# Opening of a DiT block: single first loads, plus-one by a ones matmul, scaling from PSUM, another statistics order

## The chip, the cores and the metric

The kernel runs on one core of one Trainium2 chip. The metric is the device time of one execution in microseconds (us); lower is better. The profile's "span" runs from the first to the last instruction and is about 1.8 us shorter than the device time. The engines are called PE (TensorE matmul), PEld (its weight load), DVE (VectorE), ACT (ScalarE), POOL (GpSimd) and SP (SyncE, which here issues most of the loads).

Ratios in this document are the mean time of one kernel's fast runs over the mean time of the other's fast runs of the same rounds on the same chip, so they are not quite the ratio of the medians that are quoted beside them. The bracket after a ratio is its 95% interval.

## The reference, cut to what matters

```python
B, N, D = 2, 256, 1152
mod = (silu(c) @ w_mod).reshape(B, 6, 1, D)
shift_a, scale_a, gate_a, shift_m, scale_m, gate_m = [mod[:, i] for i in range(6)]
h = layernorm(x) * (1 + scale_a) + shift_a        # the opening: this line
qkv = (h @ wqkv)...                               # K first in this kernel
...                                               # attention, wo, second norm, MLP: untouched
```

All data are bf16. The 512 tokens are four tiles of 128: tiles 0 and 1 are batch 0, tiles 2 and 3 are batch 1. The 1152 features are nine chunks of 128.

## The kernel before

x is loaded by batch, each load 576 KB. The first group of attention-scale weights (two chunks) and then rows of the K weights follow on the same queue.

```python
for b in range(B):
    nc.sync.dma_start(x_sb[:, b * TPB:(b + 1) * TPB, :], x_v[:, b, :, :])
...
for g, (k0, k1) in enumerate(KGROUPS):            # (0,2) (2,4) (4,6) (6,9)
    load_scale_group(g, nc.sync)
    for k in range(k0, k1):
        nc.sync.dma_start(w_k[:, k, 0:KM1 * P], wqkv_v[:, k, D:D + KM1 * P])
```

DVE computes the statistics of tiles 0, 2 and 3 in three pieces each. ACT computes those of tile 1 by two passes over it (Identity, then Square). The normalised tile is transposed on PE into PSUM and scaled on its way out by 1 + scale; the result feeds the K matmuls. The scale itself comes from 18 small matmuls into a PSUM tile `pm`, and ACT adds the one:

```python
def scale_group(g):
    ...
    for j in range(k0, k1):
        for k in range(KD):
            nc.tensor.matmul(pm[:, j - k0, :], w_scale_a[...], sT[:, k, 0:B],
                             start=(k == 0), stop=(k == KD - 1))
    def add_one(eng):
        ...
        nc.scalar.activation(dst, pm[:], ACT.Identity, bias=one_t[:])
```

The instructions are written in the order in which each engine is to take them (`"a"` is ACT, `"d"` is DVE; `warm(n)` issues n matmuls on zeros, whose result nobody reads, so that PE is not idle):

```python
warm(12, pwarm)
act_stats(ACT.Identity, dsum)                     # ACT, tile 1
for j in range(NPD):
    stats_piece(0, j)                             # DVE, tile 0
sqrt1(0)                                          # ACT
act_stats(ACT.Square, dsq)                        # ACT, tile 1
stats_piece(2, 0)
recip1(0)
norm1(0, 0, CUT, "d")
stats_piece(2, 1)
pt_0 = transpose_x([0, 1], [0])
warm(4, pwarm)
act_stats_finish()
sqrt1(T_ACT)
stats_piece(2, 2, False)
recip1(1)
norm1(1, 0, CUT, "d")
stats_aggregate(2)
norm1(0, CUT, D, "d")
scale_group(0)("a")
for k in range(2):
    modulate(pt_0, k, k, 0, 0, P, "a")
warm(1, pwarm)
...                                               # transposes of tile 1 and of chunks 2, 3
k_step(0, 0, P)                                   # K matmuls on tile 0
k_step(1, 0, P)
stats_piece(3, 0)
recip1(2)
norm1(2, 0, CUT, "d")
k_step(0, P, N)                                   # K matmuls on tile 1
k_step(1, P, N)
...
for k in range(2):
    transpose_into(pt_1, 6 + k, k, 2)             # transposes of tile 2
```

## Time and profile before

| | before |
|---|---|
| device time, median (range, runs) | 244.01 us (243.85 to 244.24, 3) |
| span in the profile | 242.1 us |
| PE busy | 235.3 us, 97% of the span |
| first scale weights landed | 9.09 us |
| first K matmul | 10.49 us |
| first matmul of the full-width K panels (the "mark" below) | 26.26 us |

From the page of the kernel before: the busy time of each engine, the granted PE clock in 40 slices (9 is full speed), the shares of the chain that ended last, and the group of K matmuls of the opening (count, busy us, mean ns of one, idle before).

```profile
PE 235.3 (97%) x1698; PEld 142.7 (59%) x1698; DVE 93.4 (39%) x209; ACT 69.5 (29%) x138; POOL 32.0 (13%) x48
...
PEclk9999999999999999999999999999999999999999
...
PE 91%; DMA 3%; ACT 2%; DVE 2%; issue 0%; SPq 0%; DVEq 0%
...
L288 PE MATMUL pk<-big,w_k 128*128 128x128 bf16 (+2 forms) x102 | 13.3, 278 | 0.0
```

PE bounds the kernel. A change to the opening can therefore only slide everything behind it. How the opening hangs together is seen in the chain of waits of the kernel before, in order of time (start us, duration us, what).

```profile
1.66 7.42 DMA w_scale_a<-in_w_mod_dram
...
9.13 0.62 PE pm L248 x18
...
9.77 0.27 ACT scale_a L258
...
10.07 0.64 ACT big L275 x2
10.71 0.47 DVE big L273 x2
11.17 0.47 DVE stats L188
...
11.74 0.42 DVE xn L235
...
12.21 0.28 PE pt L358 x2
12.49 0.43 PE pm L248 x18
...
12.95 1.94 PE pk L288 x21
```

The weights' landing at 9.09 us comes first, then the scale matmuls, plus-one, scaling of chunks, a piece of DVE statistics, and from 12.21 us PE runs on. The timeline of the same kernel (start us, duration us, engine, line, operation, out<-in, count, and in brackets the idle time before it and what ended it) has the DVE side.

```profile
4.79 1.48 DVE L188 BATCH_NORM_STATS2 stats<-x_sb 128x6 f32<-128x384 bf16 x3 [3.64 <-DMA x_sb<-in_x_dram]
5.05 1.24 ACT L203 ACTIVATE xn<-x_sb 128x1152 bf16<-128x1152 bf16 x1
...
6.58 0.29 ACT L219 ACTIVATE rstd<-mv,eps_t 128x1 f32<-128x1 f32 x1 [0.19 <-DVE mv L193]
...
8.95 0.41 DVE L235 TENSOR_SCALAR xn<-x_sb,mv,rstd 128x512 bf16<-128x512 bf16 x1
...
9.13 0.60 PE L248 MATMUL pm<-sT,w_scale_a 128*128 128x2 bf16 x18 [0.41 <-DMA w_scale_a<-in_w_mod_dram]
...
10.09 0.49 PE L358 MATMUL pt<-ident,xn 128*128 128x128 bf16 x6
...
10.49 1.50 PE L288 MATMUL pk<-big,w_k 128*128 128x128 bf16 x24
...
12.21 0.28 PE L358 MATMUL pt<-ident,xn 128*128 128x128 bf16 x2 [0.22 <-DVE xn L235]
```

The first statistics wait for x at 4.79 us. Tile 1 is normalised at 8.95 us, before the weights land. Within the opening, the longest wait of PE after 10.5 us is the 0.22 us before tile 2's transposes.

### The profile page before, as it was taken

To read this page: it belongs to the slowest core of one execution; us is meant where nothing else is said; L and a number is where in the kernel's file an instruction comes from. 1 tells how busy PE (TensorE), PEld (TensorE's weight loads), DVE (VectorE), ACT (ScalarE), POOL (GpSimd) and SP (SyncE) were. 2 spreads that over 40 slices of the span, in tenths; PEclk is the share of its full clock that TensorE was granted. 3 is DMA by queue.
4 is the path that set the end of the run, shared out by engine and by line. 5 is a ranking of instruction groups with operands and counts; after the bars stand their busy time and mean duration, and the time that the engine had idled before them with its cause. 6 is when DMAs were issued, how large, how long until landed. Compare 5 with 4: busy or idle time off the path is not lost.

```text
span 242.1 us, 4031 instructions
## 1 busy us (share of the span) xinstructions
PE 235.3 (97%) x1698; PEld 142.7 (59%) x1698; DVE 93.4 (39%) x209; ACT 69.5 (29%) x138; POOL 32.0 (13%) x48
## 2 busy tenths in 40 slices
PE   8799999999999999999999999999999999999994
PEld 2486444466656666888844444444566656665573
DVE  2872550675694676720000019999002000000001
ACT  6532250543735174782222233322000000000000
POOL 1000400000310616300000000000314111111111
PEclk9999999999999999999999999999999999999999
DMA  6999999999999999799999999996891000000000
GB/s 223 324 330 360 379 344 247 326 372 284 254 322 361 380 255 208 208 219 327 327 328 249 191 274 328 327 326 188 245 286 39 19 16 16 20 20 27 19 19 16
DMA packets 76989, 54.48 MB, mean 225 GB/s; under 512 B 26011, under 2 KB 72491, under 8 KB 76971
## 3 DMA queue, kind: packets, MB, share of 16 engines
q1 hardware_dynamic: 76240, 53.02, 77.7%
q0 software_dynamic: 704, 1.20, 1.6%
q8 instruction: 13, 0.21, 0.4%
q14 instruction: 5, 0.04, 0.0%
q10 hardware_dynamic: 27, 0.00, 0.0%
HBM read 46.90 MB, written 1.19 MB: 199 GB/s over the span
## 4 chain that ended last, share of the span: by engine, by line
PE 91%; DMA 3%; ACT 2%; DVE 2%; issue 0%; SPq 0%; DVEq 0%
PE pacc L866 29%; PE pacc L802 29%; PE pacc L584 7%; PE pacc L705 6%; PE pacc L511 5%; PE pk L288 4%; DMA w_scale_a<-in_w_mod_dram 3%; PE pacc L519 2%; PE pk L318 2%; ACT hT L687 2%; PE pa L619 1%; PE ps_s L539 1%; PE pn L432 1%; PE pm L248 1%; PE pt L266 1%; PE pg L467 1%
## 5 line engine op out<-in xcount | busy, mean ns | idle before, releaser
L802 PE MATMUL pacc<-hT,w_f 128*128 128x256 bf16 (+1 forms) x432 | 70.5, 326 | 0.2 <-ACT hT L687 0.2
L866 PE MATMUL pacc<-w_f,gT 128*128 128x384 bf16 (+2 forms) x468 | 70.5, 314 | 0.0
L866 PEld LDWEIGHTS <-gT 128*128 128x128 bf16 x468 | 44.4, 98 | 26.2
L802 PEld LDWEIGHTS <-w_f 128*128 128x128 bf16 x432 | 42.2, 98 | 28.0 <-issue 0.4
L485 DVE SCALAR_TENSOR_TENSOR late<-w_gate_mT,late 128x1152 bf16<-128x1152 bf16 x18 | 24.4, 1358 | 36.8 <-DMA w_gate_mT<-in_w_mod_dram 36.2
L872 DVE TENSOR_TENSOR tmp<-pacc,gate 128x384 f32<-128x384 f32 (+2 forms) x13 | 6.8, 527 | 62.5 <-PE pacc L866 50.5
L840 ACT ACTIVATE gT<-pacc 128x512 bf16<-128x512 f32 x24 | 14.3, 597 | 32.3 <-PE pacc L802 32.3
L485 DVE SCALAR_TENSOR_TENSOR s_spill<-w_scale_m,s_b 128x1152 bf16<-128x1152 bf16 x12 | 16.3, 1357 | 8.5 <-DMA w_scale_m<-in_w_mod_dram 8.2
L705 PE MATMUL pacc<-w_o,big 128*128 128x384 bf16 (+2 forms) x117 | 17.9, 314 | 0.0
L874 POOL TENSOR_TENSOR o_sb<-tmp,x 128x384 bf16<-128x384 f32 (+1 forms) x12 | 11.7, 974 | 47.4 <-DVE tmp L872 47.4
L584 PE MATMUL pacc<-w_v,hT 128*128 128x384 bf16 x108 | 17.9, 326 | 0.0
L705 PEld LDWEIGHTS <-big 128*128 128x128 bf16 x117 | 11.0, 98 | 6.8 <-ACT big L627 0.2
L584 PEld LDWEIGHTS <-hT 128*128 128x128 bf16 x108 | 10.4, 98 | 7.0 <-issue 0.2
L288 PE MATMUL pk<-big,w_k 128*128 128x128 bf16 (+2 forms) x102 | 13.3, 278 | 0.0
L711 POOL TENSOR_TENSOR x<-tmp,x_sb 128x384 f32<-128x384 f32 (+1 forms) x11 | 9.8, 891 | 17.4 <-DVE tmp L710 9.5
L511 PE MATMUL pacc<-hT,w_q 128*128 128x512 bf16 x54 | 11.8, 379 | 0.1
L327 POOL DMA_DIRECT2D gates_dram<-grow x4 | 2.1, 521 | 70.8 <-DVE grow L826 70.8
L818 ACT ACTIVATE gT<-pacc 128x512 bf16<-128x512 f32 x12 | 6.9, 597 | 10.4 <-PE pacc L802 10.4
L288 PEld LDWEIGHTS <-w_k 128*128 128x128 bf16 x102 | 7.8, 98 | 3.0
L511 PEld LDWEIGHTS <-w_q 128*128 128x128 bf16 x54 | 5.3, 98 | 6.7 <-issue 0.4
L710 DVE TENSOR_TENSOR tmp<-pacc,gate 128x384 f32<-128x384 f32 (+2 forms) x13 | 6.7, 522 | 5.4 <-PE pacc L705 5.2
L523 ACT ACTIVATE big<-pacc 128x512 bf16<-128x512 f32 x9 | 4.8, 608 | 11.5 <-PE pacc L511 8.8
(101 smaller groups left out, 160.9 us busy)
## 6 DMA issues: line engine op xcount, KB each, us to landing
w_f<-in_w_fc_dram SPq DMA_DIRECT2D x14, 864.0 KB, 11.0
w_f<-in_w_fc_dram SPq DMA_DIRECT2D x2, 2592.0 KB, 10.7
w_f<-in_w_fc_dram SPq DMA_DIRECT2D x2, 1728.0 KB, 13.8
w_shift_a<-in_w_mod_dram SPq DMA_DIRECT2D x3, 864.0 KB, 10.5
w_v<-in_wqkv_dram SPq DMA_DIRECT2D x3, 864.0 KB, 6.0
w_gate_a<-in_w_mod_dram SPq DMA_DIRECT2D x3, 864.0 KB, 9.2
w_o<-in_wo_dram SPq DMA_DIRECT2D x3, 864.0 KB, 6.2
w_shift_m<-in_w_mod_dram SPq DMA_DIRECT2D x3, 864.0 KB, 13.0
```

What stands on the lines that cost most here:

```text
L288: nc.tensor.matmul(pk[m][:, c0:c1], w_k[:, k, m * P:(m + 1) * P], hT0[:, k, c0:c1], start=(k == 0 and c0 == 0), stop=(k == KD - 1), skip_g ...
L485: nc.vector.scalar_tensor_tensor(spill, wT[:, j, :], 1.0, s_b[b], op0=ALU.mult, op1=ALU.mult, accum_out=dst(j, b),)
L511: nc.tensor.matmul(pq[m][:], w_q[:, k, m * P:(m + 1) * P], hT[:, k, :], start=(k == 0), stop=(k == KD - 1),)
L584: nc.tensor.matmul(pacc[:], hT[:, k, t * P:(t + 1) * P], w_v[:, k, pnl * PW:(pnl + 1) * PW], start=(k == 0), stop=(k == KD - 1),)
L705: nc.tensor.matmul(pacc[:], aT[:, k, t * P:(t + 1) * P], w_o[:, k, c0:c1], start=(k == ks[0]), stop=(k == ks[-1]),)
L711: (nc.vector if (t, i) in ((1, 2), (3, 3)) else nc.gpsimd).tensor_tensor(x1[:, t, c0:c1], tmp[:], x_sb[:, t, c0:c1], op=ALU.add)
L802: nc.tensor.matmul(dst, w_f1[m // KD][:, k, ml * P:(ml + 1) * P], hT[:, k, c0:c1], start=(k == 0), stop=(k == KD - 1),)
L818: nc.scalar.activation(gT[:, ms[0]:ms[-1] + 1, b * N:(b + 1) * N], pacc[:], ACT.Gelu_apprx_tanh)
L840: nc.scalar.activation(gT[:, m, :], pacc[:], ACT.Gelu_apprx_tanh)
L866: nc.tensor.matmul(pacc[:], gT[:, kk, t * P:(t + 1) * P], w_f2[j][:, r, c0 - n * PW:c0 - n * PW + cw], start=(kk == 0), stop=(kk == KF - 1),)
L872: nc.vector.tensor_tensor(tmp[:], pacc[:], gate_m[:, b, c0:c0 + cw], op=ALU.mult)
L874: (nc.vector if last else nc.gpsimd).tensor_tensor(o_sb[:], tmp[:], x1[:, t, c0:c0 + cw], op=ALU.add)
```

## The change

The intent is to start the statistics of tile 0 earlier, because its half of the load lands first; to take ACT's plus-one out of the chain by seeding the PSUM tile with ones, so that the scale matmuls add onto them; and to let DVE scale the first chunks straight from that PSUM tile instead of waiting for ACT's copy. The order of statistics, transposes and K matmuls was rearranged with it.

```diff
@@ -81,8 +81,9 @@
     x_sb = act.tile([P, NT, D], BF16, name="x_sb", tag="x_in")
     c_sb = act.tile([B * KD, P], BF16, name="c_sb")
     nc.scalar.dma_start(c_sb[:], c_v)
-    for b in range(B):
-        nc.sync.dma_start(x_sb[:, b * TPB:(b + 1) * TPB, :], x_v[:, b, :, :])
+    for l in range(TPB):
+        nc.sync.dma_start(x_sb[:, l, :], x_v[:, 0, l, :])
+    nc.sync.dma_start(x_sb[:, TPB:NT, :], x_v[:, 1, :, :])
 
     zeros = const.tile([P, T], BF16, name="zeros")
     nc.vector.memset(zeros[:], 0.0)
@@ -90,8 +91,8 @@
     make_identity(nc, ident[:])
     eps_t = const.tile([P, 1], FP32, name="eps_t")
     nc.vector.memset(eps_t[:], LN_EPS)
-    one_t = const.tile([P, 1], FP32, name="one_t")
-    nc.vector.memset(one_t[:], 1.0)
+    ones_r = const.tile([1, P], BF16, name="ones_r")
+    nc.vector.memset(ones_r[:], 1.0)
     SW = 32
     sT = act.tile([P, KD, SW], BF16, name="sT")
     nc.gpsimd.memset(sT[:], 0.0)
@@ -240,24 +241,36 @@
 
     scale_a = act.tile([P, KD, B], FP32, name="scale_a")
 
-    def scale_group(g):
+    def scale_group_matmuls(g):
         k0, k1 = KGROUPS[g]
         pm = aux_tile([P, k1 - k0, B], "pm")
+        nc.tensor.matmul(
+            pm[:].rearrange("p j b -> p (j b)"), ones_r[:, 0:P], ones_r[:, 0:(k1 - k0) * B], start=True, stop=False,
+            skip_group_check=True,
+        )
         for j in range(k0, k1):
             for k in range(KD):
                 nc.tensor.matmul(
                     pm[:, j - k0, :], w_scale_a[:, k, j * P:(j + 1) * P], sT[:, k, 0:B],
-                    start=(k == 0), stop=(k == KD - 1),
+                    start=False, stop=(k == KD - 1), skip_group_check=True,
                 )
 
-        def add_one(eng):
+        return pm
+
+    def scale_group_copy(g, pm):
+        k0, k1 = KGROUPS[g]
+
+        def copy_out(eng):
             dst = scale_a[:, k0:k1, :]
             if eng == "d":
-                nc.vector.tensor_scalar_add(dst, pm[:], 1.0)
+                nc.vector.tensor_copy(dst, pm[:])
             else:
-                nc.scalar.activation(dst, pm[:], ACT.Identity, bias=one_t[:])
-
-        return add_one
+                nc.scalar.copy(dst, pm[:])
+
+        return copy_out
+
+    def scale_group(g):
+        return scale_group_copy(g, scale_group_matmuls(g))
 
     def transpose_x(ks, ts, pt=None, js=None):
         pt = aux_tile([P, len(ks), len(ts) * P], "pt", BF16) if pt is None else pt
@@ -330,28 +343,27 @@
 
     CUT = 4 * P
     warm(12, pwarm)
-    act_stats(ACT.Identity, dsum)
     for j in range(NPD):
         stats_piece(0, j)
+    act_stats(ACT.Identity, dsum)
     sqrt1(0)
     act_stats(ACT.Square, dsq)
-    stats_piece(2, 0)
     recip1(0)
     norm1(0, 0, CUT, "d")
-    stats_piece(2, 1)
+    for j in range(NPD):
+        stats_piece(2, j)
     pt_0 = transpose_x([0, 1], [0])
     warm(4, pwarm)
     act_stats_finish()
     sqrt1(T_ACT)
-    stats_piece(2, 2, False)
+    sqrt1(2)
+    stats_piece(3, 0)
     recip1(1)
     norm1(1, 0, CUT, "d")
-    stats_aggregate(2)
-    norm1(0, CUT, D, "d")
-    scale_group(0)("a")
+    pm_0 = scale_group_matmuls(0)
     for k in range(2):
-        modulate(pt_0, k, k, 0, 0, P, "a")
-    warm(1, pwarm)
+        nc.vector.tensor_scalar_mul(hT0[:, k, 0:P], pt_0[:, k, 0:P], pm_0[:, k, 0:1])
+    nc.scalar.copy(scale_a[:, 0:2, :], pm_0[:])
     pt_1 = aux_tile([P, 1, 8 * P], "pt", BF16)
 
     def transpose_into(pt, slot, k, t):
@@ -359,39 +371,41 @@
 
     for k in range(2):
         transpose_into(pt_1, k, k, 1)
-    for k in (2, 3):
-        for t in range(TPB):
-            transpose_into(pt_1, 2 * (k - 1) + t, k, t)
+    recip1(2)
+    norm1(2, 0, CUT, "d")
     for k in range(2):
-        modulate(pt_1, 0, k, 1, k * P, P, "d")
-    sqrt1(2)
+        modulate(pt_1, 0, k, 1, k * P, P, "a")
     k_step(0, 0, P)
     k_step(1, 0, P)
-    stats_piece(3, 0)
-    recip1(2)
-    norm1(2, 0, CUT, "d")
-    k_step(0, P, N)
-    k_step(1, P, N)
     stats_piece(3, 1)
     stats_piece(3, 2)
     for k in range(2):
         transpose_into(pt_1, 6 + k, k, 2)
+    k_step(0, P, N)
+    for k in (2, 3):
+        for t in range(TPB):
+            transpose_into(pt_1, 2 * (k - 1) + t, k, t)
+    k_step(1, P, N)
     for k in range(2):
         modulate(pt_1, 0, k, 2, (6 + k) * P, P, "a")
-    scale_group(1)("a")
     sqrt1(3)
-    for k in (2, 3):
-        modulate(pt_1, 0, k, 0, 2 * (k - 1) * P, N, "d")
     k_step(0, N, N + P)
-    k_step(1, N, N + P)
+    pm_1 = scale_group_matmuls(1)
     recip1(3)
     norm1(3, 0, CUT, "d")
+    for k in (2, 3):
+        nc.vector.tensor_scalar_mul(
+            hT0[:, k, 0:N], pt_1[:, 0, 2 * (k - 1) * P:2 * k * P], pm_1[:, k - 2, 0:1]
+        )
+    nc.scalar.copy(scale_a[:, 2:4, :], pm_1[:])
+    k_step(1, N, N + P)
     k_step(2, 0, N)
     k_step(3, 0, N, 0, 3)
     pt_4 = transpose_x([0, 1], [3])
     for k in range(2):
         modulate(pt_4, k, k, 3, 0, P, "d")
     k_step(3, 0, N, 3, KM1)
+    norm1(0, CUT, D, "d")
     norm1(1, CUT, D, "d")
     pt_5 = transpose_x([2, 3], [2, 3])
     for i, k in enumerate((2, 3)):
```

In words, for the order: DVE now does all of tile 2's statistics before those of tile 1 are finished; the two scalings of tile 0 go to DVE and those of tile 1 to ACT; and in PE's own queue the transposes of tile 2 move ahead of tile 1's K matmuls, and the four transposes of chunks 2 and 3 come between those K matmuls.

## The prediction

> **What bounds the kernel now.** TensorE. The page of before has PE busy 235.3 of 242.1 us, and 91% of the chain of waits is PE. The change touches only the opening. In the timeline PE does useful work without a gap from 12.2 us on, so every later stage simply slides with the opening. What can be won lies before that. In the chain the opening is: the first attention-scale weights land at 9.09 us (3.1% of the span); the scale matmuls run 9.13 to 9.73; ACT adds one (9.77 to 10.03) and scales two chunks (10.07 to 10.69); the first K matmuls start at 10.49; a DVE statistics, reciprocal and normalise piece holds PE idle 0.22 us until 12.21. The first matmul on chunk 2 comes at about 13.70 (12 K matmuls after 12.95). I compare that point, because the same PE work lies before it in both kernels.
>
> **What changes.**
> 1. x tile 0 lands alone. Half of a 576 KB load that landed at 4.75 us should land near 3.9. But the square root that tile 0 needs still stands on ACT behind the 1.24 us Identity pass over tile 1, which cannot start before 5.05 us (table load). So the root moves only from 6.58 to about 6.40: 0.18 us gained; DVE idles over a microsecond. The one more issue (0.41 us on SP) shifts the weights little: the DMA share is already near full there.
> 2. The plus-one goes to a ones matmul (tens of ns, ahead of the weights' landing for the first group; about 0.05 us each for later groups). The seeding is legal by the Trainium skill, "PSUM — Partial Sum Buffer", The four PSUM rules: matmuls without the first flag accumulate onto it. No run so far shows it.
> 3. DVE scales chunks 0 and 1 straight from PSUM. That takes ACT's 0.26 us out of the chain. But DVE now runs all three pieces of tile 2 (1.5 us) and their aggregate before tile 1's statistics. From root at 6.40: reciprocal 6.72, normalise 6.92, pieces 7.25 to 8.77, aggregate, three small operations 8.9 to 9.3, a tile 3 piece, reciprocal 9.8, normalise tile 1 9.97 to 10.38 (before: 8.95 to 9.36), the two scalings 10.30 to 10.78. So DVE, not the weights, ends the wait.
> 4. In the built program the tile 1 transposes, ahead of the K matmuls on PE, wait for those DVE scalings (buffer reuse); ACT's copy of the scale waits for DVE too, and tile 2's transposes wait for ACT's scalings of tile 1. I estimate first K matmul 10.95 (before 10.49), tile 2 transposes 11.8, scale group 1 at 13.4, chunk 2 at 14.1 to 14.4.
>
> **Sum.** +0.4 to +0.7 us at the comparison point, +0.1 for later ones matmuls, minus what my DVE chain overstates. The rest slides. I put it at +0.4 us: **244.4 us**, 8 in 10 between 243.7 and 244.9. Faster by over 2%: 1%; within 2%: 98%; slower by over 2%: 1%.
>
> **What would show it.** Timeline of after: first statistics near 3.9 instead of 4.79; DVE idle between tile 0's aggregate and its reciprocal near 6.7; normalise of tile 1 near 10.0; first K matmul later than 10.49; no ACT plus-one; PE continuous from about 13.4. All PE groups after 15 us unchanged in duration.
>
> **What would make it wrong.** Tile 0's square root getting in front of the Identity pass, which would pull the DVE chain forward by about a microsecond and give a gain of up to 0.5 us; x tile 1 landing after 5.05 us, or the scale weights after 10.3, which costs more; waits finer than I read them (tile 2's scalings released early), which brings the loss near zero.

## More of the kernel before

The mark is useful because all K work of the opening lies before it in both kernels and almost nothing after it changes.

The six transposes of tile 1 and of chunks 2 and 3 run at 10.09 us, ahead of the first K matmul, while PE waits for the scaled chunks.

## The result and the profile after

| | before | after |
|---|---|---|
| device time, median (range, runs) | 243.93 us (243.63 to 244.24, 4) | 246.79 us (246.53 to 246.98, 4) |
| span in the profile | 242.1 us | 245.2 us |
| first statistics | 4.79 us | 3.80 us |
| batch 1 of x landed | 6.22 us | 8.46 us |
| first scale matmul | 9.13 us | 10.49 us |
| first K matmul | 10.49 us | 12.12 us |
| the mark | 26.26 us | 29.60 us |

The ratio is 1.0116 [1.0099, 1.0134]. The loss is about 2.8 us where +0.4 us was predicted, and 246.79 us lies outside the predicted range. The mark moved by 3.34 us, and the first MLP matmul, far behind it, moved by 3.23 us (98.75 to 101.98 us): the loss is made in the opening, and the rest slides.

From the page of the kernel after: the engines, the granted clock and the group of K matmuls that answers to the one shown of before.

```profile
PE 237.5 (97%) x1701; PEld 144.5 (59%) x1701; DVE 93.8 (38%) x209; ACT 69.2 (28%) x138; POOL 31.9 (13%) x48
...
PEclk9979999999999999999999999999999999999999
...
L301 PE MATMUL pk<-big,w_k 128*128 128x128 bf16 (+2 forms) x102 | 14.7, 297 | 0.0
```

PE's busy time grew by 2.2 us with three more matmuls. Part of that is the same K matmuls taking longer (13.3 to 14.7 us), and the third slice of the clock shows a 7. The chain of waits of this execution reaches back only to 92.56 us, so the opening is read from the timeline of the kernel after.

```profile
3.80 1.48 DVE L189 BATCH_NORM_STATS2 stats<-x_sb 128x6 f32<-128x384 bf16 x3 [2.53 <-DMA x_sb<-in_x_dram]
...
4.98 1.24 ACT L204 ACTIVATE xn<-x_sb 128x1152 bf16<-128x1152 bf16 x1
...
6.53 0.16 DVE L223 RECIPROCAL rstd<-rstd 128x1 f32<-128x1 f32 x1 [0.98 <-ACT rstd L220]
...
8.48 1.48 DVE L189 BATCH_NORM_STATS2 stats<-x_sb 128x6 f32<-128x384 bf16 x3 [1.34 <-DMA x_sb<-in_x_dram]
...
10.49 0.60 PE L253 MATMUL pm<-sT,w_scale_a 128*128 128x2 bf16 x18 [1.90 <-DMA w_scale_a<-in_w_mod_dram]
...
11.15 0.41 DVE L236 TENSOR_SCALAR xn<-x_sb,mv,rstd 128x512 bf16<-128x512 bf16 x1
11.48 0.48 DVE L365 TENSOR_SCALAR big<-pt,pm 128x128 bf16<-128x128 bf16 x2
...
12.01 0.27 PE L370 MATMUL pt<-ident,xn 128*128 128x128 bf16 x2 [0.92 <-DVE big L365]
...
12.04 0.16 ACT L366 COPY scale_a<-pm 128x4 f32<-128x4 f32 x1 [1.02 <-DVE rstd L223]
...
12.12 0.83 PE L301 MATMUL pk<-big,w_k 128*128 128x128 bf16 x12
```

Three things are to be seen. The statistics of tile 0 do start earlier (3.80 us), and nothing comes of it: DVE waits 0.98 us for the root at 6.53 us, which stands on ACT behind the pass over tile 1. Then DVE waits 1.34 us for batch 1 of x, until 8.48 us, and PE waits 1.90 us for the scale weights, until 10.49 us: two landings that were predicted to stay where they were. And tile 1's normalisation (11.15 us) and the two DVE scalings stand between the scale matmuls and the first K matmul at 12.12 us. Of the two late landings it is batch 1's that counts in this execution: from 8.48 us until its scalings start at 11.48 us DVE goes from one instruction to the next with no wait over 0.1 us, and the scale matmuls had ended before that, at 11.09 us.

What the landing looked like, from the semaphore increments of the 16 DMA engines in the two traces (us, one number per increment; weights: first and last ones only):

```
before  batch 1 of x: 5.49 ... 5.91  6.08  6.22
before  scale weights: 7.57 ... 8.56  9.09
after   batch 1 of x: 5.39 5.44 5.49 5.50 5.52 5.53 5.54 5.56 5.80 5.84 5.89 6.04 6.09 7.42 8.29 8.46
after   scale weights: 7.37 ... 9.36  10.28  10.44
```

Thirteen of the 16 engines were done by 6.09 us; three came 1.3 to 2.4 us later, and the load counts as landed only with the last. The Trainium skill says so too, "DMA: Bandwidth & Descriptors", Why a DMA increments its semaphore by 16 and not by 1: only the full 16 means that all data landed; this trace agrees, DVE started at 8.48 us, 0.02 us after the sixteenth increment. While batch 1 was moving, two single 4608-byte packets took 1316 ns (started at 5.01 us) and 1519 ns (5.21 us), where the median is 178 ns. The trace does not name the engine of a packet, so that these two ran on late engines is not shown.

The granted clock is read in windows of 1 us. The columns are the window's start and end (us), its length, the busy share and count of PE, PEld, DVE, ACT and POOL, then the granted clock, the DMA share and GB/s. First the kernel before:

```profile
13.00:14.00 1.00, 1.00 (x15) 0.88 (x15) 0.97 (x5) 0.60 (x3) 0.00 (x0) 1.00 1.15 312
14.00:15.00 1.00, 1.00 (x13) 0.91 (x11) 0.44 (x2) 0.00 (x0) 0.00 (x0) 1.00 1.07 350
```

The windows of the kernel after:

```profile
9.00:10.00 1.00, 0.00 (x0) 0.00 (x0) 0.97 (x4) 0.00 (x0) 0.00 (x0) 1.00 1.13 339
...
11.00:12.00 1.00, 0.09 (x4) 0.10 (x1) 0.96 (x6) 0.03 (x1) 0.00 (x0) 1.00 1.01 293
...
13.00:14.00 1.00, 0.94 (x11) 0.94 (x11) 0.64 (x2) 0.00 (x1) 0.00 (x0) 0.62 1.17 316
14.00:15.00 1.00, 1.00 (x13) 1.00 (x10) 0.00 (x0) 0.61 (x3) 0.00 (x0) 0.50 1.01 313
15.00:16.00 1.00, 1.00 (x19) 0.79 (x18) 0.57 (x2) 0.20 (x2) 0.00 (x0) 0.50 1.00 310
16.00:17.00 1.00, 1.00 (x21) 0.97 (x19) 0.62 (x2) 0.00 (x0) 0.00 (x0) 0.67 1.03 320
```

PE is idle from 8.6 to 12.0 us but for the 0.60 us of scale matmuls, and from about 13.2 us it gets half its clock. If the clock is 1.00 or 0.50 and nothing between, the four shares make 0.76 + 1 + 1 + 0.66 = 3.42 us at half speed; one window laid over 13.24 to 16.66 us gives 0.50 for the whole of it. The Trainium skill, "TensorE: Matmul & The Clock Gate", Part 1: The HAM clock gate, describes this: a PE that was idle for a window of about 3.4 us gets 4 of 8 clock pulses until it has been busy for about 3.4 us, and the window runs freely, so that it varies between runs. The length and the factor agree with this trace. The condition does not quite: the longest waits of PE here are 1.90 and 0.92 us, and none is 3.4 us long.

### The profile page after: what moved, and what is told of

Read it like the earlier page. It is cut to its first block, busy times and chain, and to the rows that moved or that the text cites. A ratio compares the mean times of both kernels' runs of the same rounds, so it can differ in the third digit from the quotient of the medians.

```text
span 245.2 us, 4041 instructions
## 1 busy us (share of the span) xinstructions
PE 237.5 (97%) x1701; PEld 144.5 (59%) x1701; DVE 93.8 (38%) x209; ACT 69.2 (28%) x138; POOL 31.9 (13%) x48
## 4 chain that ended last, share of the span: by engine, by line
PE 57%; ACT 2%; DMA 1%; issue 0%; DVE 0%; ACTq 0%; DVEq 0%
PE pacc L880 29%; PE pacc L816 28%; ACT hT L701 2%; DMA hT<-xn 1%; ACT xn L680 0%; ACT rstd L671 0%; DVE tmp L886 0%; DVE o_sb L888 0%; ACTq L701 0%; DVEq L886 0%
## 5 line engine op out<-in xcount | busy, mean ns | idle before, releaser
L301 PE MATMUL pk<-big,w_k 128*128 128x128 bf16 (+2 forms) x102 | 14.7, 297 | 0.0
L301 PEld LDWEIGHTS <-w_k 128*128 128x128 bf16 x102 | 8.7, 107 | 2.8
L172 PE MATMUL pwarm<-zeros 128*128 128x512 bf16 x20 | 7.2, 524 | 1.2 <-DVE eps_t L93 1.2
## 6 DMA issues: line engine op xcount, KB each, us to landing
w_shift_a<-in_w_mod_dram SPq DMA_DIRECT2D x3, 864.0 KB, 11.1
```

The costliest lines, as they stand in the source:

```text
L172: nc.tensor.matmul(dst[:], zeros[:, 0:P], zeros[:], start=True, stop=True)
L301: nc.tensor.matmul(pk[m][:, c0:c1], w_k[:, k, m * P:(m + 1) * P], hT0[:, k, c0:c1], start=(k == 0 and c0 == 0), stop=(k == KD - 1), skip_g ...
```

## The experiments

Three theories stood against each other for the 2.8 us. *Loads*: the split first load makes batch 1 and the weights land late. *Order*: the rearranged instructions on DVE, ACT and PE are slower by themselves. *Clock*: the idle PE loses its clock. They are not exclusive, so the experiments were to size each. All kernels gave a correct result. Times are the median with range and number of fast runs; "at clock 1" means executions whose mean granted clock was 0.997 or more, and executions with the dip show 0.991 to 0.993. In each batch the kernel before was run on the same chip; its medians were 243.68, 243.79, 243.88, 243.82 and 243.63 us.

| experiment | what | median us (range, fast runs) | ratio [95%] |
|---|---|---|---|
| e1_split_only | before + split load | 245.41 (243.57 to 246.23, 6) | 1.0060 [1.0028, 1.0092] |
| e8_split_again | the same again, other chip | 244.99 (244.22 to 246.11, 4) | 1.0049 [1.0020, 1.0079] |
| e2_all_but_split | after with the loads of before | 245.65 (244.79 to 245.80, 6) | 1.0070 [1.0050, 1.0090] |
| e4_after_again | after, again | 246.41 (245.48 to 247.16, 4) | 1.0106 [1.0079, 1.0132] |
| e3_after_warm | after + warm matmuls | 245.45 (245.38 to 245.88, 5) | 1.0074 [1.0056, 1.0092] |
| e5_order_warm | e2 + warm matmuls | 245.08 (245.00 to 245.24, 6) | 1.0050 [1.0034, 1.0067] |
| e6_old_stats | e2, nearly old statistics order, warm | 245.27 (245.03 to 245.96, 6) | 1.0059 [1.0039, 1.0079] |
| e10_ones_only | before + ones matmul | 244.07 (243.87 to 244.40, 6) | 1.0008 [0.9990, 1.0026] |
| e11_stats_order_only | before + statistics order | 244.12 (243.76 to 244.23, 6) | 1.0007 [0.9990, 1.0023] |
| e9_psum_scale_old_order | before + ones + scaling from PSUM | 244.09 (243.82 to 244.90, 6) | 1.0015 [0.9995, 1.0034] |
| e13_pe_order_only | before + PE order | 244.75 (244.40 to 245.58, 6) | 1.0032 [1.0007, 1.0056] |
| e14_old_pe_order | e2 with the PE order of before | 244.97 (244.56 to 245.53, 5) | 1.0039 [1.0016, 1.0062] |
| e12_split_batch1 | before, batch 1 split | 244.00 (243.84 to 244.26, 4) | 1.0006 [0.9987, 1.0026] |
| e7_partition_halves | before, batch 0 in two halves of partitions | 245.06 (244.81 to 246.11, 4) | 1.0057 [1.0031, 1.0083] |
| e15_weights_first | before, weights ahead of batch 1 | 245.87 (244.32 to 246.67, 6) | 1.0072 [1.0039, 1.0104] |
| e16_split_weights_first | the same with batch 0 split | 244.79 (244.29 to 246.19, 6) | 1.0044 [1.0016, 1.0071] |

### Loads and order apart: e1, e2, e8

e1 and e8 are the kernel before with the change's loads alone:

```diff
-    for b in range(B):
-        nc.sync.dma_start(x_sb[:, b * TPB:(b + 1) * TPB, :], x_v[:, b, :, :])
+    for l in range(TPB):
+        nc.sync.dma_start(x_sb[:, l, :], x_v[:, 0, l, :])
+    nc.sync.dma_start(x_sb[:, TPB:NT, :], x_v[:, 1, :, :])
```

> The kernel before with only the x load of batch 0 split in two, everything else as before. Theory D (the extra transfer upsets the opening transfers: in the trace of after, batch 1 of x landed at 8.48 us instead of before 6.46, the first scale weights at 10.44 instead of 9.09): batch 1 lands after 8 us and the weights after 10 us here too, and the time is 245.0 to 246.0 us. Rival O (the loss is the new instruction order, the late landings are chance or harmless): batch 1 by 6.8 us, the weights by 9.5 us, time within 0.3 us of before. A rival in between: only the 0.47 us of the extra issue shows, time +0.3 to +0.5 us.

(The 8.48 and 6.46 us in this text are the starts of DVE's first work on batch 1; the landings are 8.46 and 6.22 us.)

> The kernel before with only the load split by tile, once more, for a second trace. Its times were 243.57 to 246.23 us and the trace fell on the fastest execution. If the late landing is what makes the slow ones: a trace of 244.8 us or more shows batch 1 after 7.3 us or the weights after 9.4 us; a fast one shows neither. If slow executions show loads as early as before, the landing is not the cause.

e2 is the kernel after with that edit taken back.

> The changed kernel with the two x loads of before; all else changed. My prediction's sum (order alone): first K matmul near 10.95 us, time +0.4 to +0.7 us against before. Theory D alone: no loss, time within 0.3 us of before. If order is the whole loss (rival O): +2.5 to +3 us and a clock dip near 13 us although the loads land as before.

Both parts lose. The split alone gave 1.0060 and 1.0049, with a wide spread: in e1 from 243.57 to 246.23 us, that is from no loss at all to nearly the whole one. Three of e1's six executions and one of e8's four had the clock dip, which no execution of the kernel before had in these rounds: the split alone can bring it on. The profile of e1 fell on its fastest execution, where batch 1 landed at 6.95 us and the weights at 9.01 us; it shows little, which is why e8 was run. The timeline of e8 shows the late landing in a kernel whose instructions are those of before:

```profile
7.52 0.56 DVE L189 BATCH_NORM_STATS2 stats<-x_sb 128x6 f32<-128x384 bf16 x1 [2.09 <-DMA x_sb<-in_x_dram]
```

DVE waits 2.09 us for batch 1. Fifteen of the 16 engines had landed it by 5.85 us, the last at 7.50 us. Tile 1 is normalised at 10.03 us (before 8.95), the first K matmul comes at 10.98 (10.49), and the mark stands at 26.76 us, 0.50 later than before, where batch 1 was 1.28 us late: there is slack behind the landing. The expectation for e8 was missed all the same. It had late landings in slow executions alone, and this one, the fastest of the four (244.22 us), has one. No trace of a slow execution of e1 or e8 was taken, so it is not shown that the slow ones are those whose loads land latest.

e2, without the split, still gave 1.0070. Its timeline normalises tile 1 at 9.71 us (before: 8.95), and waits for DVE before PE goes on:

```profile
10.04 0.48 DVE L364 TENSOR_SCALAR big<-pt,pm 128x128 bf16<-128x128 bf16 x2
...
10.57 0.27 PE L369 MATMUL pt<-ident,xn 128*128 128x128 bf16 x2 [0.94 <-DVE big L364]
10.61 0.16 ACT L365 COPY scale_a<-pm 128x4 f32<-128x4 f32 x1 [1.02 <-DVE rstd L222]
```

That is the DVE chain of the prediction. ACT's copy starts after the DVE scalings, though it only reads the same PSUM tile that DVE reads; the Trainium skill, "PSUM — Partial Sum Buffer", PSUM bank collisions raise a hardware error, says that two engines' accesses to the same bank and quadrant have to be ordered, ACT against DVE and reads included, and this trace shows such an order (the scalings end at 10.52 us, the copy starts at 10.61).

But five of e2's six executions also show the clock dip. Its windows:

```profile
10.00:11.00 1.00, 0.43 (x8) 1.00 1.15 313
11.00:12.00 1.00, 1.00 (x14) 0.56 1.09 339
```

(These two are for PE alone, so after PE's busy share come the clock, the DMA share and GB/s.) The one execution of e2 that kept its clock took 244.79 us, the five others 245.5 to 245.8, on average 0.9 more.

### The clock: e3, e4, e5

e3 is the kernel after with eight more warm matmuls in the gap, which PE would otherwise idle through. e4 is the kernel after again, in the same batch.

```diff
-    warm(4, pwarm)
+    warm(12, pwarm)
     act_stats_finish()
```

> The changed kernel with 12 instead of 4 warm-up matmuls while PE waits for the first scale weights, so that PE stays busy from 7.4 to about 10.1 us. Theory C (part of the loss is the granted clock: 0.50 to 0.67 from 13.4 to 16.7 us in the trace of after, following an idle PE from 8.6 to 12.0): clock 1.0 throughout 12 to 20 us and about 0.8 to 1.3 us faster than the changed kernel (245.5 to 246.0 us). Rival (the clock dip costs nothing, as PE waits for DVE there): within 0.3 us of 246.8.

> The changed kernel once more, for a second trace. If the late landing of batch 1 of x (8.48 us) and of the weights (10.44 us) belongs to the program, they are within 0.5 us of that again, and the time is 246.5 to 247.0 us; if it was chance of one execution, batch 1 lands near 6.5 us in this trace although the time is the same.

e4 gave 1.0106 and repeats the result; three of its four executions had the dip (246.25 to 247.16 us), the fourth kept its clock and took 245.48. e3 gave 1.0074, and all its fast executions had a clock of 0.999 or more. Filling the gap, which adds work that nobody needs, so made the kernel about 0.8 us faster ((1.0106 - 1.0074) x 243.7). The two intervals overlap, but the size agrees with the 0.9 us between the executions of e2 with and without the dip. One execution of e3, the profiled one, took 358.56 us at a mean clock of 0.659; it is left out, and the trace of e3 is not used for more.

One caution: of the kernel after itself, one of the four executions kept its clock and still took 246.60 us. Executions differ in their landings as well, so single ones prove little; the sizes are taken from means over a kernel.

e5 is e2, so with the loads of before, and with warm matmuls in both gaps: the order alone, without late loads and without the dip.

```diff
-    warm(4, pwarm)
+    warm(8, pwarm)
     act_stats_finish()
...
     pm_0 = scale_group_matmuls(0)
+    warm(3, pwarm)
```

> The changed kernel with the x loads of before (so the weights land near 9.0 us) and 7 more warm-up matmuls in PE's idle stretches around the first scale group, so that the granted clock stays at 1. It isolates the instruction order without clock dip and without late landing. In the run with the loads of before but no extra warm-ups the one execution with clock 1.000 took 244.79 us, the others (clock 0.992) 245.5 to 245.8. Theory (order costs about 1.1 us, the dip about 0.9 us): this run is +0.9 to +1.3 us against before, with all executions at clock 0.998 or above. Rival (the dip is the whole loss of that run): within 0.3 us of before.

It gave 1.0050 with the smallest spread of all (245.00 to 245.24 us), at a clock of 0.998 to 1.0. So the order costs about 0.0050 x 243.8 = 1.2 us. In its timeline the clock does not dip and the first K matmul still comes late:

```profile
10.08 0.41 DVE L235 TENSOR_SCALAR xn<-x_sb,mv,rstd 128x512 bf16<-128x512 bf16 x1
10.41 0.48 DVE L365 TENSOR_SCALAR big<-pt,pm 128x128 bf16<-128x128 bf16 x2
...
11.05 0.83 PE L300 MATMUL pk<-big,w_k 128*128 128x128 bf16 x12
...
12.10 0.50 PE L300 MATMUL pk<-big,w_k 128*128 128x128 bf16 x6
...
12.44 0.39 PE L370 MATMUL pt<-ident,xn 128*128 128x128 bf16 x4
```

Tile 1 is normalised at 10.08 us and the first K matmul comes at 11.05; the prediction had 9.97 and 10.95. The mark stands at 27.69 us, 1.43 us later than before. The prediction's comparison point, the first matmul on chunk 2, comes at 14.86 us (before 13.75): 1.11 us later, of which 0.57 us is the first K matmul and 0.55 us the stretch between the two (rounded; 3.81 us, before 3.26). In that stretch PE is not waiting much longer than before: it is busy 3.49 of 3.81 us, before 3.02 of 3.26. It has more to do: the four transposes of chunks 2 and 3, which ran in the wait before the first K matmul, stand between K matmuls now and put them off by 0.22 us (12.44 to 12.66), and a ones matmul puts off what follows by 0.11 us. The other 0.2 us lies in short breaks between these groups of matmuls.

### Which part of the order: e6, e9, e10, e11, e13, e14

e10 has the ones matmul and a plain ACT copy in place of ACT's plus-one, and nothing else:

```diff
+        nc.tensor.matmul(pm[...], ones_r[:, 0:P], ones_r[...], start=True, stop=False, ...)
...
-                    start=(k == 0), stop=(k == KD - 1),
+                    start=False, stop=(k == KD - 1), skip_group_check=True,
...
-                nc.scalar.activation(dst, pm[:], ACT.Identity, bias=one_t[:])
+                nc.scalar.copy(dst, pm[:])
```

> The kernel before with only the plus-one moved into a ones matmul, the ACT addition becoming a copy. One chain link shortens by about 0.1 us (the ACT addition took 0.26 us, the copy takes 0.16), three ones matmuls in a busy stream cost 0.05 to 0.1 us each: time within 0.3 us of before. If seeding has a hidden cost, +0.5 us or more.

ACT's copy takes 0.16 us where the plus-one took 0.26, and the first K matmul comes at 10.24 us instead of 10.49 in the profiled execution. The time is 1.0008, not distinguishable from no change: the mark stands at 26.35 us (before 26.26), so the gain of the first matmul is given back before it. Of the 0.25 us only 0.10 is the change's: in this execution the weights landed at 8.94 us, 0.15 earlier than in the one of before. The result is correct, as in all kernels with the seeding; this is the rule of the Trainium skill's "PSUM — Partial Sum Buffer", The four PSUM rules, which the prediction relied on, and the runs agree with it.

e11 has the statistics order of the change alone:

```diff
-    stats_piece(2, 0)
     recip1(0)
     norm1(0, 0, CUT, "d")
-    stats_piece(2, 1)
+    for j in range(NPD):
+        stats_piece(2, j)
...
-    stats_piece(2, 2, False)
     recip1(1)
     norm1(1, 0, CUT, "d")
-    stats_aggregate(2)
```

> The kernel before with only the statistics reordered: three pieces and aggregate of tile 2 ahead of tile 1's finish. From the durations of the trace: tile 1's normalise moves from 8.95 to 9.7 us, its transposes from 10.09 to about 10.2, first K matmul near 10.6; +0.1 to +0.4 us. If the statistics order were the main cost of the change (rival): +0.8 us or more.

Tile 1 is normalised at 9.64 us instead of 8.95, and the time is 1.0007: by itself this is hidden, because ACT is busy with its plus-one and the scaling of tile 0 until then, and the first K matmul comes at 10.57 us.

e9 has the ones matmul and DVE's scalings from PSUM, with the statistics and the PE order of before:

```diff
-    scale_group(0)("a")
-    for k in range(2):
-        modulate(pt_0, k, k, 0, 0, P, "a")
+    pm_0 = scale_group_matmuls(0)
+    for k in range(2):
+        nc.vector.tensor_scalar_mul(hT0[:, k, 0:P], pt_0[:, k, 0:P], pm_0[:, k, 0:1])
+    nc.scalar.copy(scale_a[:, 0:2, :], pm_0[:])
...
-        modulate(pt_1, 0, k, 1, k * P, P, "d")
+        modulate(pt_1, 0, k, 1, k * P, P, "a")
```

> The loads, the statistics order and the PE order of before; of the change only the ones matmul and the scaling of chunks 0 to 3 of batch 0 straight from PSUM. The run with the old statistics order but the changed PE order had its first K matmul at 10.46 us and still cost +1.3 us; PE stood 0.77 us before tile 2's transposes, which the changed order puts ahead of tile 1's K matmuls, and 12 K matmuls later its tile 2 scalings waited for four more transposes. Theory P (the changed PE order is the cost): here first K matmul near 10.5 to 10.7 us, no PE gap over 0.3 us after it, time within 0.4 us of before. Rival S (the scaling from PSUM itself, by holding both buffers until DVE is done, is the cost): +0.8 us or more again.

1.0015, again not clear of no change. Its profile fell on its slowest execution (244.90 us), in which one DMA engine brought batch 1 late (15 by 5.86 us, the last at 7.56 us, the weights at 9.50) although nothing is split here. So late engines also occur without the split.

e13 has only the new PE order on the kernel before: tile 2's transposes ahead of tile 1's K matmuls, the transposes of chunks 2 and 3 between those, the second scale group later.

```diff
-    for k in (2, 3):
-        for t in range(TPB):
-            transpose_into(pt_1, 2 * (k - 1) + t, k, t)
...
-    k_step(0, P, N)
-    k_step(1, P, N)
...
     for k in range(2):
         transpose_into(pt_1, 6 + k, k, 2)
+    k_step(0, P, N)
+    for k in (2, 3):
+        for t in range(TPB):
+            transpose_into(pt_1, 2 * (k - 1) + t, k, t)
+    k_step(1, P, N)
```

> The kernel before with only PE's order of the change: tile 2's transposes ahead of tile 1's K matmuls, the four transposes of chunks 2 and 3 between those, scale group 1 after the first K matmuls of tile 2. DVE and ACT work as before, no scaling from PSUM. If PE's order is the cost: a PE gap of 0.5 us or more appears before tile 2's transposes, and time is +0.7 to +1.3 us. If it costs only together with the scaling from PSUM (which makes tile 1's scalings late): +0.1 to +0.4 us.

1.0032, and 244.40 to 244.92 us in the four executions at clock 1, on average 0.6 us over the mean of before in that batch (244.59 against 243.97); the other two had the dip and took 245.37 and 245.58. This part alone is slower, and its timeline shows how. The profile fell on an execution with the dip, which begins at 11.72 us, so the times after that are stretched by the clock too:

```profile
10.10 0.83 PE L288 MATMUL pk<-big,w_k 128*128 128x128 bf16 x12
...
11.59 0.31 PE L358 MATMUL pt<-ident,xn 128*128 128x128 bf16 x2 [0.66 <-DVE xn L235]
...
12.34 0.63 PE L358 MATMUL pt<-ident,xn 128*128 128x128 bf16 x4
...
13.01 0.63 ACT L275 ACTIVATE big<-pt,scale_a 128x128 bf16<-128x128 bf16 x2 [2.52 <-PE pt L358]
```

PE finishes tile 0's K matmuls at 10.93 us and then stands 0.66 us behind tile 2's transposes, which wait for DVE. Tile 1's scalings ended at 10.56 us, so its 12 K matmuls were ready all that time; they stand behind the transposes in PE's queue. Then ACT's scalings of tile 2 start only at 13.01 us, when the four extra transposes into the same PSUM tile are done (12.97), where before they started at 12.53. The second scale group's scaling on DVE slipped from 13.34 to 15.05 us. How much of these two delays is the order and how much the clock, this trace cannot tell; the 0.66 us are before the dip.

e14 is the other half: all of the order except PE's, which is that of before.

```diff
     for k in range(2):
         transpose_into(pt_1, k, k, 1)
+    for k in (2, 3):
+        for t in range(TPB):
+            transpose_into(pt_1, 2 * (k - 1) + t, k, t)
...
+    k_step(0, P, N)
+    k_step(1, P, N)
     for k in range(2):
         transpose_into(pt_1, 6 + k, k, 2)
```

> The changed kernel with the loads of before and with PE's order of before for the first K matmuls, transposes and scale group 1; statistics order, scaling from PSUM and ones matmul as changed, warm-ups as changed. Without the restored order this was +1.9 us (245.65, mostly with the clock dip) and +1.2 us without dip. If PE's order is the cost: within 0.5 us of before. If it is not: +1 us or more.

1.0039, with 244.56 to 244.98 us in four executions at clock 1, on average 0.9 us over the mean of before, between the two outcomes that were expected. Against the 1.2 us of the whole order (e5), taking PE's order back wins 0.2 to 0.4 us, and the intervals of the two overlap. One more execution, the profiled one, took 876.44 us; it is left out and its trace is not used.

e6 has the PE order and the PSUM scaling with nearly the statistics order of before, and warm matmuls:

```diff
-    for j in range(NPD):
-        stats_piece(2, j)
+    stats_piece(2, 0)
     recip1(0)
     norm1(0, 0, CUT, "d")
+    stats_piece(2, 1)
...
-    warm(4, pwarm)
+    warm(7, pwarm)
...
     nc.scalar.copy(scale_a[:, 0:2, :], pm_0[:])
+    stats_piece(2, 2)
+    sqrt1(2)
```

> As e5_order_warm (loads of before, warm-ups), but with the DVE statistics in nearly the order of before: tile 1's normalise ahead of tile 2's last piece and aggregate; the scaling straight from PSUM and the ones matmul stay. If the three pieces and the aggregate ahead of tile 1 are the cost of the order: tile 1's normalise starts by 9.2 us, the first K matmul by 10.5 us, time within 0.4 us of before. If the cost is in the buffer and bank waits that the scaling from PSUM brings (transposes behind DVE, ACT's copy behind DVE, ACT's scalings behind the extra transposes): first K matmul early, but a PE gap before the second tile's K matmuls stays, and time is +0.7 us or more.

1.0059: taking the statistics order back does not help. Tile 1 is normalised at 8.64 us and the first K matmul comes at 10.46, as before, but PE then waits 0.77 us for DVE before tile 2's transposes.

So the parts do not add up: ones matmul 1.0008, statistics 1.0007, ones and PSUM scaling 1.0015, PE order 1.0032, statistics with PSUM scaling 1.0039, PE order with PSUM scaling 1.0059, all 1.0050. The PE order is the only part that costs clearly by itself. The later statistics and the scaling from PSUM cost nothing that is seen when alone and about 0.9 us together (e14): each seems to be hidden by slack that the other uses up. That is a reading of the ratios; the intervals of e5, e6 and e14 overlap, and where that slack lies was not measured part by part.

### Why the loads come late: e12, e7, e15, e16

e12 splits batch 1 instead of batch 0, so the queue also has three x transfers, but its head is the old one:

```diff
+    nc.sync.dma_start(x_sb[:, 0:TPB, :], x_v[:, 0, :, :])
+    for l in range(TPB):
+        nc.sync.dma_start(x_sb[:, TPB + l, :], x_v[:, 1, l, :])
```

> The kernel before with batch 1 of x instead of batch 0 split by tile: three x transfers, 2304-byte packets in the second and third. If a third x transfer as such makes the landings late and unsteady (first scale weights after 9.3 us): time +0.5 to +2 us, spread over 1 us. If only small packets at the head of the queue do it: weights by 9.2 us, time within 0.4 us of before.

1.0006 and steady. A third transfer, and the issue of it, cost nothing that is seen; the last x transfer landed at 6.73 and the weights at 8.65 us. It matters which load is split, as far as four executions and one trace can say.

e7 splits batch 0 by partitions, so that rows stay 4608 bytes:

```diff
+    nc.sync.dma_start(x_sb[0:64, 0:TPB, :], x_v[0:64, 0, :, :])
+    nc.sync.dma_start(x_sb[64:P, 0:TPB, :], x_v[64:P, 0, :, :])
```

> The kernel before with batch 0 of x loaded in two transfers of 64 partitions each (packets of 4608 bytes as before, three x transfers as in the change). If the number of transfers unsettles the opening: batch 1 lands after 6.9 us and the time is as unsteady as with the split by tile (243.6 to 246.2 us). If it is the packets of 2304 bytes: batch 1 near 6.3 us, time within 0.4 us of before and steady.

This was inconclusive. The packets of the halves took about 300 to 350 ns instead of 178, the first statistics started only at 6.04 us and the weights landed at 9.69; a different loss hides what was asked. Batch 1 came late here with all its engines (6.84 to 7.58 us), not with a few of them.

e15 puts batch 1 behind the first scale weights, with tile 2's statistics later; e16 does that and splits batch 0.

```diff
         load_scale_group(g, nc.sync)
+        if g == 0:
+            nc.sync.dma_start(x_sb[:, TPB:NT, :], x_v[:, 1, :, :])
```

> The kernel before with batch 1 of x loaded behind the first scale weights, and tile 2's statistics moved behind tile 1's scalings so that DVE does not wait for it. The scale weights should land near 7.5 us instead of 9.09; the first K matmul is then bound by the first rows of w_k (9.6 us in before), near 9.8 us instead of 10.49. If the opening is bound by the scale weights: -0.3 to -0.7 us. If later landings (second scale group at 12.2 us, needed at 12.33) bind as soon as PE is ahead: within 0.3 us of before.

> As e15_weights_first, with batch 0 of x split by tile. If whatever follows the split loads is hit: the last engine of the first scale weights comes 0.8 us or more behind the one that is in the middle, the weights land after 8.3 us, and time is +0.5 us or more over e15 and unsteady. If batch 1's packets of 4608 bytes behind those of 2304 are what is hit: weights near 7.5 us as in e15, batch 1 late, and time within 0.4 us of e15.

e15 was also a try at a faster kernel. It gave scale matmuls at 8.28 us and the first K matmul at 9.62 us, 0.87 us earlier than before, and a ratio of 1.0072:

```profile
12.99 0.29 PE L355 MATMUL pt<-ident,xn 128*128 128x128 bf16 x2 [1.87 <-DVE xn L236]
```

PE then waits 1.87 us for tile 2, and four of six executions had the dip (245.86 to 246.67 us, against 244.32 and 244.40). Both traces show packets of about 0.9 to 1.3 us again, in e15 with no split at all and around 5.5 us, when the weights are moving. In e16 six of the 16 engines held back the weights (6.86 to 8.18 us, the others by 6.41). That suggests that it is not batch 1 as such that comes late, but whatever moves at 5 to 6 us. The ratio of e16, 1.0044, lies below e15's, so the further 0.5 us that was one expectation did not come; and e15, which was expected to gain or to be equal, lost.

What makes a packet long stays open. What the traces show is this: with the head load split, batch 1 landed between 6.95 and 8.46 us in each of four profiled executions (after, e1, e4, e8; e3's slow one not counted), against 5.94 to 6.22 in seven of eight with the x loads of before (7.56 in the eighth, e9). No edit was found that changes the packets' timing alone, so why a split head load goes with late engines was not tested further.

## Why the prediction was right or wrong

The sum, from means: the order alone costs about 1.2 us (e5). Late landings add about 0.6 us (e3 over e5: (1.0074 - 1.0050) x 243.7); the six executions of e1 and e8 at clock 1 average 244.6 us, 0.8 over the mean of before, so 0.6 to 0.8. The dip adds 0.8 to 1.0 us (e4 and after, 1.0106 and 1.0116, over e3). Together 2.6 to 3.0 us, where 2.6 and 2.8 were measured. The intervals of these ratios reach 0.4 to 0.8 us to each side, e5 ran on another chip than e3 and e4, and for after the record names none, so the sizes are rough, and that they add up so well is in part luck. That each of the three is there is shown by a run in which it stood alone or was taken away: the order in e5, the loads in e1 and e8, the dip in e3.

- **Right: the earlier tile 0 gains nothing.** Statistics at 3.80 us (predicted "near 3.9"), the reciprocal at 6.53 ("near 6.7"), because the root stays behind ACT's Identity pass (4.98 to 6.22 us).
- **Right in mechanism: DVE ends the wait, not the weights.** Transposes behind DVE's scalings, ACT's copy behind DVE, tile 2's transposes behind: all in the traces. In e5, where nothing else disturbs, tile 1 is normalised at 10.08 and the first K matmul comes at 11.05 us; the prediction said 9.97 and 10.95. From tile 0's normalisation to tile 1's, DVE's chain took 2.99 us there (7.09 to 10.08), and the prediction had 3.05.
- **Mis-sized: "+0.4 to +0.7 us at the comparison point ... I put it at +0.4 us".** The order alone measured 1.2 us (e5), and 1.11 us at that point in its trace. The delay of the first K matmul was about right (0.57 us, predicted 0.46). What was mis-sized is the stretch from there to chunk 2: predicted 3.15 to 3.45 us, measured 3.81 (before 3.26). The prediction compared that point "because the same PE work lies before it in both kernels". The work is the same but for the ones matmuls; but four transposes, which cost nothing in the wait before the first K matmul, now run after it and cost their time. That ready K matmuls stand behind waiting transposes costs by itself (0.66 us idle in e13), but in e5 and after PE waits only 0.11 and 0.10 us there. In the profile after, the point is at 16.76 us in place of 13.75, with all three causes in it.
- **Wrong: "The one more issue (0.41 us on SP) shifts the weights little".** The issue does cost little (e12), but the load split at the head of the queue went with late DMA engines: batch 1 at 8.46 instead of 6.22 us and weights at 10.44 instead of 9.09. "the scale weights after 10.3" stood among what would make the prediction wrong, and it happened; it was not weighed in the sum. That batch 1 could come late was not thought of, and in this execution it is batch 1 that moved the DVE chain: tile 1 was normalised at 11.15 us, predicted 9.97.
- **Wrong: "PE continuous from about 13.4. All PE groups after 15 us unchanged in duration."** PE has half its clock from about 13.2 to 16.7 us, and the opening's K matmuls take 14.7 us in place of 13.3. PE was nearly continuous from 12.0 us, earlier than predicted; "unchanged in duration" is what failed. That a gap on PE is paid a second time through the clock was missing from the sum: 0.8 to 1.0 us.
- **Right: "within 2%"**, at 98%. The range, 243.7 to 244.9 us, was too narrow: it held only the error of the chain's sum, and no term for the landings or the clock.

No version was found that beats the kernel before. The ones matmul, the statistics order, the PSUM scaling with the old orders and the split of batch 1 each measure as equal to it.

## What to carry to other kernels

PE took its queue in order here, so an instruction that will wait must not stand in front of work that is ready (e13): look at what PE could have done in the gap, not only at what ends the gap. Work that ran in such a gap was free, and cost its full time once it was moved behind the gap (the four transposes, 0.22 us in e5). A stretch in which PE idled in part for some 3 us cost its own length and, in most executions, again through the granted clock; eight matmuls on zeros were worth about 0.8 us. A landing is as late as the slowest of its DMA engines, so after a change to the first loads look at the increments one by one and at the spread over several executions, and before shortening one wait find out which wait ends last.

## What the Trainium skill lacked or had wrong

- "DMA: Bandwidth & Descriptors" (the two sections on queues and semaphores): it says that the engines of one DMA finish independently, but these sections give no size for how far apart. Here, in the opening, single packets took 1.0 to 1.5 us where the median of those of 4608 bytes is 178 ns, and one to three engines of 16 landed up to 2.4 us after the others (6.09 against 8.46 us). With the head load split, batch 1 was late in each of four profiled executions (6.95 us and more); without the split a late engine also occurred (e9), and long packets in e15. Its cause is open.
- The same page, Rules for kernel authors, advises against two transfers to the two halves of the partitions, because they use the same engines, and gives no size. In e7 their packets took about 300 to 350 ns against 178, and the ratio was 1.0057.
- "TensorE: Matmul & The Clock Gate", Part 1: the two states and the 3.4 us agree (0.50 for 3.42 us). Its table names an idle window of about 3.4 us as the condition, and a later section of the same Part short idle stretches between groups of matmuls, without a size; here the clock dropped when PE was not wholly idle. In e2, PE was busy 0.45, 0.60 and 0.43 in the three windows from 8 to 11 us, and the dip began at about 11.1. One execution of six of the same kernel had none, which fits the page's word that it varies from run to run. How much idle time is enough, no run here tells, and the busy share alone does not decide it: in e13 PE was busy 2.38 of the 3.41 us before the dip (8.31 to 11.72), and e4's profiled execution, with 1.43 of 3.40 us (8.50 to 11.90), kept its clock.
- No page that I read has the rare long executions: 358.56 us at a mean clock of 0.659 (e3) and 876.44 us (e14), once each.
